# Mamba2 scan and PReLU block: pairs 2 to 5 in the half-and-half layout, and the last group's product 3 unsplit

## The chip, the cores and the metric

The kernel runs on one core of a Trainium2 chip. The metric is the device time of one execution in microseconds. The core's engines are TensorE (PE, with its weight loads as PEld), VectorE (DVE), ScalarE (ACT), GpSimd (POOL) and SyncE (SP, which here only issues transfers); sixteen DMA engines move data. Each engine has its own queue of instructions and waits for others by semaphores.

## The reference

Two stages follow each other. The first is a state-space scan with batch 4, 8 heads, 768 tokens, head size 32 and state size 16. The second takes the scan's result as 3072 tokens of 256 values through a hidden layer of 2048 with a two-sided PReLU.

```python
# first stage, per batch and head (run in chunks in the reference)
state = decay[t] * state + outer(B[t], x[t])
y[t]  = C[t] @ state
# bridge: (B,H,S,D) -> (B*S, H*D)
x = attn_out.transpose(0, 2, 1, 3).reshape(3072, 256)
h = x @ w_in                                       # 256 x 2048
g = np.maximum(h, 0.0) + alpha * np.minimum(h, 0.0)
return g @ w_out                                   # 2048 x 256
```

In chunked form a chunk's output is (C B^T, times a triangle of decays) x, plus the decayed C times the state at the chunk's start. The weights arrive in 64-bit floats.

## The kernel before

**Chunks and pairs.** The kernel uses chunks of Q = 128 tokens, 6 per batch, and works on two chunks at a time: pairs gp = 0 to 11, three per batch. For each pair it loads B, C and x (`nat`, `xt`), decays spread over partitions (`abc`, from rows that the kernel itself writes to a scratch in DRAM) and cumulated decays (`ap`). For one pair the steps are: transposes of B and C (`T`, L640), the products C B^T called gram (L702, L713), triangles of decays by scans on DVE (L532, L538), their product with gram (L724), the pair's share to the two states called added (L580, L595), the update of the states with a mask on POOL (L613, L616), and y (L750 to L758, L768 to L776), which ACT copies into `xT`, the tokens of the second stage.

**Two layouts.** Pairs 0 to 5 hold a whole chunk on all 128 partitions, one after the other. Pairs 6 to 11 (`gp >= HALF`) hold chunk k on half k of the partitions, in two blocks of 64 tokens. There the triangle needs only 192 columns per head (SQ) in place of 256, gram, y and added issue their matmuls in two halves of TensorE's rows, B and x are loaded in four transfers of 64 partitions (`load_tokens`, L146), and parts of C and the state have to be moved to the other half of the partitions (`moved`, L656, ACT L661 and POOL L663). The layout also wants the decay rows turned in a halved form: `rows_turn` (L443, copies at L457) does it for the second set of rows, which serves pairs 6 to 11. The first set, for pairs 0 to 5, is turned whole.

**Groups.** The second stage works on groups of 512 tokens, which are two pairs. Group 0 (pairs 0 and 1) is computed plainly by `hidden` (L996, ACT L999) and `output` (L1034) over 16 slices f of the hidden layer, while the weights arrive and are converted in pieces: raw on SP (L249), wt and wg on ACT (L265, L272, L275), POOL L267, DVE L286 and L296, and POOL L318 writes the finished piece. Its first four slices run as `hidden_two` (L1011) inside `first_two` (L792), the function that computes pairs 0 and 1. Groups 1 to 5 use a scheme of seven products in place of eight: `quad` (L1118) issues the first product (L1130), PReLU (L1113, L1115) and the second product (`product`, L1105), and calls `after(j)` between its steps.

**Order.** The order is written out by hand. Pairs 2 and 3 run in coarse steps within the loop over f from 4 to 15 of group 0; pairs 4 to 11 run in fine steps that `after(j)` places by its dictionary of steps in the quads. `load_next` and `load_pair` place the transfers on SP's queue, where pair 2's loads stand ahead of the fifth and later weight pieces. `keep_warm` (L326) issues matmuls of ones on TensorE, at the very start and where it would wait in `first_two`.

**State products.** For pairs 4 to 11, added of pair gp + 1 is put into unused columns of the banks of pair gp's y (`beside`). For pairs 2 and 3 it has a bank of its own and is issued ahead of gram, at the first of the coarse steps.

**The end.** In the last group, product 3 is computed with tokens on the partitions (L1097), in four matmuls of 128 columns per call and in two halves. `close` (L1218) then issues the products as 1, 2, 6, 5, 7, 4 and the halves of 3, with transposes (L1229) between them; the part `rest` that needs product 3 is transposed ahead of it, two adds on DVE (L1273) finish it, and `send` (L1235) stores each half in 64 KB.

## Time and profile before

| What | us |
|---|---|
| Three runs: lowest, median, highest | 359.12, 359.5, 359.89 |
| Profiled execution: its time and its span | 359.5, 357.8 |
| PE busy of the span | 350.7 (98%) |
| PEld | 288.2 (81%) |
| DVE | 239.4 (67%) |
| POOL | 205.3 (57%) |
| ACT | 173.7 (49%) |

The span is the time from the first to the last event of the profile; 1.7 us lie around it. The slices show each engine's busy share in tenths over 40 equal parts of the span. In a timeline a row gives the start, the time, the engine, the line, the operation with output and input, the shapes and how many instructions follow each other; in brackets is the idle time of the engine before it and what ended it. A group of matmuls is pipelined, so a row's end overlaps the next row's start.

### The profile page before, as it was taken

Reading aid. Unit: us, or ns where it says so; the run is one execution under the profiler, and the core shown is the slowest. Engines: PE = TensorE matmul, PEld = TensorE weight load, DVE = VectorE, ACT = ScalarE, POOL = GpSimd, SP = SyncE. Lnnn points to the kernel's source line nnn. Section 1 sums busy time; section 2 is a strip of 40 time slices with the busy share of each in tenths; the row PEclk is TensorE's granted clock in tenths of the full one; section 3 lists DMA queues with packets and bytes.
Section 4 is the critical chain, followed back from the end, with each engine's and each line's share of the span. In section 5 each row is a group of like instructions: output and inputs, shape, how many; then the busy total and the mean of one; then the engine's idle time right before and its main releaser. Section 6 shows DMA issues by size and latency. Waiting matters only on the chain.

```text
span 357.8 us, 7565 instructions
## 1 busy us (share of the span) xinstructions
PE 350.7 (98%) x2894; PEld 288.2 (81%) x2894; DVE 239.4 (67%) x467; ACT 173.7 (49%) x387; POOL 205.3 (57%) x221
## 2 busy tenths in 40 slices
PE   8899999999999999999999999999999999999995
PEld 7576666578888888888888888888888888888884
DVE  6987986998748756857747847757856633653263
ACT  3577666535355346346345445445445344444331
POOL 4886668589938855725645725647626535533520
PEclk9999999999999999999999999999999999999999
DMA  6989999508245403503413423413001002002004
GB/s 112 191 178 310 319 217 242 136 16 170 93 92 127 96 2 74 105 2 80 92 38 75 84 54 74 88 48 72 3 4 29 0 2 31 0 0 32 0 3 88
DMA packets 105469, 30.19 MB, mean 84 GB/s; under 512 B 79880, under 2 KB 101336, under 8 KB 105432
## 3 DMA queue, kind: packets, MB, share of 16 engines
q1 hardware_dynamic: 104360, 29.39, 37.3%
q8 instruction: 23, 0.38, 0.5%
q10 hardware_dynamic: 1072, 0.31, 0.4%
q14 instruction: 14, 0.11, 0.1%
HBM read 26.32 MB, written 3.37 MB: 83 GB/s over the span
## 4 chain that ended last, share of the span: by engine, by line
PE 85%; SPq 7%; DVE 3%; DMA 1%; ACT 1%; POOL 1%; issue 1%; ACTq 0%; DVEq 0%
PE bank L1105 32%; PE hp L1130 28%; PE bank L1034 6%; PE ss L1130 6%; PE hp L996 3%; SPq L188 3%; SPq L192 2%; PE ss L758 1%; DMA raw<-in_moe_w_in_dram 1%; DVE dec L538 1%; PE ss L702 1%; PE bank L1097 1%; PE ss L750 1%; PE ss L776 1%; DVE wr L296 1%
## 5 line engine op out<-in xcount | busy, mean ns | idle before, releaser
L1187 POOL TENSOR_TENSOR gt<-gt 128x512 f32<-128x512 f32 x58 | 74.2, 1278 | 21.1 <-DVE gt L1115 16.3
L1105 PE MATMUL bank<-gt,w_out 128*128 128x256 f32 x320 | 83.8, 382 | 0.2 <-DVE u L1248 0.2
L1105 PEld LDWEIGHTS bank<-gt,w_out 128*128 128x128 f32 x320 | 60.0, 190 | 9.7 <-issue 1.6
L1115 DVE SCALAR_TENSOR_TENSOR gt<-hp,s_mul,gt 128x256 f32<-128x256 f32 x96 | 42.0, 479 | 29.1 <-ACT gt L1113 26.9
L1177 POOL TENSOR_TENSOR gt<-gt 128x512 f32<-128x512 f32 x20 | 25.4, 1269 | 62.6 <-DVE gt L1115 50.2
L1113 ACT ACTIVATE gt<-hp,s_alpha 128x256 f32<-128x256 f32 x96 | 40.3, 471 | 34.6 <-PE hp L1130 31.5
L1105 PE MATMUL bank<-gt,ws 128*128 128x256 f32 x224 | 55.9, 379 | 0.0
L1105 PEld LDWEIGHTS bank<-gt,ws 128*128 128x128 f32 x224 | 42.3, 190 | 5.6
L1130 PE MATMUL hp<-xs,w_in 128*128 128x256 f32 x160 | 41.9, 384 | 0.0
L1130 PE MATMUL hp<-xs,ws 128*128 128x256 f32 x160 | 41.1, 380 | 0.0
L1156 DVE TENSOR_TENSOR hp<-hp,u 128x512 f32<-128x512 f32 x20 | 14.0, 700 | 35.8 <-ACT u L1154 35.8
L1130 PEld LDWEIGHTS hp<-xs,ws 128*128 128x128 f32 x160 | 30.3, 190 | 4.3 <-POOL xs L1075 0.2
L1130 PEld LDWEIGHTS hp<-xs,w_in 128*128 128x128 f32 x160 | 29.7, 190 | 4.4
L1034 PE MATMUL bank<-w_out,gt 128*128 128x256 f32 x128 | 31.1, 385 | 0.1
L1034 PEld LDWEIGHTS bank<-w_out,gt 128*128 128x128 f32 x128 | 23.6, 190 | 6.9 <-issue 2.9
L1130 PE MATMUL ss<-xT,w_in 128*128 128x256 f32 x96 | 24.6, 379 | 0.0
L996 PE MATMUL hp<-xT,w_in 128*128 128x512 f32 x48 | 22.7, 596 | 0.1
L616 POOL TENSOR_TENSOR sm<-state,bmask 128x256 f32<-128x256 f32 (+1 forms) x10 | 6.2, 619 | 28.9 <-DVE state L613 28.9
L532 DVE TENSOR_TENSOR_SCAN dec<-abc,bank 128x192 f32<-128x192 f32 x48 | 22.7, 523 | 0.0
L1145 ACT COPY m<-hp 128x512 f32<-128x512 f32 x8 | 4.7, 586 | 35.7 <-PE hp L1130 35.7
L1154 ACT COPY u<-hp 128x512 f32<-128x512 f32 x20 | 11.7, 586 | 19.4 <-PE hp L1130 19.4
L1115 DVE SCALAR_TENSOR_TENSOR gt<-c,s_mul,gt 128x256 f32<-128x256 f32 x40 | 20.5, 554 | 0.0
(204 smaller groups left out, 617.4 us busy)
## 6 DMA issues: line engine op xcount, KB each, us to landing
abc<-z SPq DMA_DIRECT2D x24, 192.0 KB
raw<-in_moe_w_in_dram SPq DMA_DIRECT2D x8, 512.0 KB
raw<-in_moe_w_out_dram SPq DMA_DIRECT2D x8, 512.0 KB
abc<-z SPq DMA_DIRECT2D x8, 512.0 KB
out_dram<-o_sb SPq DMA_DIRECT2D x33, 64.0 KB
nat<-in_B_dram SPq DMA_DIRECT2D x26, 64.0 KB
nat<-in_C_dram SPq DMA_DIRECT2D x24, 64.0 KB
xt<-in_x_dram SPq DMA_DIRECT2D x12, 128.0 KB
```

Of the source, the lines that this page charges most:

```text
L188: nc.sync.dma_start(out=nat[:, i, k].rearrange("p (h n) -> p h n", h=H), in_=src[b, :, ts, :].rearrange("h p n -> p h n"))
L532: nc.vector.tensor_tensor_scan(out=dv[:, o : o + SQ], data0=abc[k][:, s : s + SQ], data1=ident_p[0][:, :SQ], initial=0.0, op0=ALU.mult, op ...
L996: nc.tensor.matmul(hp, w_in[:, k, f * P : (f + 1) * P], xts[g][:, k], start=(k == 0), stop=(k == KC - 1))
L1034: nc.tensor.matmul(pos[0][t // 2][:, t % 2], gt[:, t * Q : (t + 1) * Q], w_out[:, f], start=(f == 0 and t % 2 == 0), stop=(f == NF - 1), s ...
L1105: nc.tensor.matmul(ms[g][i][:, h], w, blocks[g, z][n][:, p], start=(q == 0 and h == 0), stop=(q == NQ - 1), skip_group_check=True)
L1113: nc.scalar.mul(o[:, p], h[:, p], s_alpha[:, fs[p]])
L1115: nc.vector.scalar_tensor_tensor(out=o[:, p], in0=h[:, p], scalar=s_mul[:, fs[p]], in1=o[:, p], op0=ALU.mult, op1=ALU.max)
L1130: nc.tensor.matmul(to[:, p], w(2 * z + p), b, start=start and p == 0, stop=True, skip_group_check=True)
L1154: nc.scalar.copy(out=u2, in_=A)
L1156: nc.vector.tensor_tensor(out=Y, in0=Y, in1=u2, op=ALU.add)
L1177: nc.gpsimd.tensor_tensor(out=tc_, in0=g22, in1=g12, op=ALU.subtract)
L1187: eng.tensor_tensor(out=o, in0=x0, in1=x1, op=ALU.subtract)
```

## The change

Pairs 2 to 5 take the layout of pairs 6 to 11; pairs 0 and 1 stay whole, with a loader of their own (`load_whole`).

- Loads: B and x of pairs 2 to 5 in four transfers each, the spread of decays of every later pair as two transfers into one tile of 1536 columns, which has two buffers.
- Row products: the first set is turned twice in `first_two`, whole for pairs 0 and 1 and halved for pairs 2 to 5. The halved form is written by four matmuls into the upper half of the bank `hp`, four ACT copies take it out, and four calls of `keep_warm`, in place of six, follow in the same bank. The second set is turned by four matmuls as well, so the two ACT copies that swapped its halves go. DVE copies the ends of the rows.
- The identity that the scans use is halved where it is made, ahead of pair 2, and no longer ahead of pair 6.
- Pairs 2 and 3: added stands right behind gram, in unused columns of the gram banks 2 and 3; the update of the states and the moved parts follow it.
- The transposes of B turn a token block at a time, and ACT copies them out in two parts.
- The end: product 3 is two matmuls of 256 columns per call again, as the other products are. `close` issues 1, 2, 5, 6, 7, 4, 3 without transposes between them and then three blocks of transposes, copy (ACT, ACT, DVE) and store of 128 KB; one of the sums moves to POOL.

```diff
-    lda = ctx.enter_context(tc.tile_pool(name="lda", bufs=3))
+    lda = ctx.enter_context(tc.tile_pool(name="lda", bufs=2))
...
-        for w, t in enumerate(loads["p", gp][1] if gp >= HALF else ()):
-            rows = scratch["z", b // 2].rearrange("(b h c) t -> b c h t", b=2, h=H)
-            for k in range(2):
-                nc.sync.dma_start(
-                    out=t[HQ * k : HQ * (k + 1), : 4 * SQ].rearrange("p (h t) -> p h t", h=4),
-                    in_=rows[b % 2, c + k, 4 * w : 4 * w + 4].unsqueeze(0)
-                    .to_broadcast([HQ, 4, SQ]))
-        for k, t in enumerate(loads["p", gp][1] if gp < HALF else ()):
-            rows = scratch["z", b // 2].rearrange("(b h c) t -> b c h t", b=2, h=H)[b % 2, c + k]
-            nc.sync.dma_start(out=t.rearrange("p (h t) -> p h t", h=H),
-                              in_=rows.unsqueeze(0).to_broadcast([P, H, Q]))
+        rows = scratch["z", b // 2].rearrange("(b h c) t -> b c h t", b=2, h=H)[b % 2]
+        for k in range(2):
+            nc.sync.dma_start(
+                out=loads["p", gp][1][HQ * k : HQ * (k + 1)].rearrange("p (h t) -> p h t", h=H),
+                in_=rows[c + k].unsqueeze(0).to_broadcast([HQ, H, SQ]))
...
     def load_pair(gp, decays=True):
...
+        nat, abc, xt, ap = pair_tiles(gp)
+        if gp >= NB:
+            load_heads(ap, "pf", b, c)
+        load_tokens(nat[:, 0], B[b], c * Q)
+        if gp > GC:
+            for i, src in enumerate((B, C)):
+                load_blocks(nat, i, src[b], c * Q)
+        else:
+            load_chunks(nat[:, 1], C[b], c * Q)
+        load_tokens(xt, x[b], c * Q)
+        if decays:
+            load_spread(gp, b, c)
...
         nc.scalar.copy(out=m5_bank[0][:, HT:], in_=ident_h[:, :HT])
+        for s in range(2):
+            nc.scalar.copy(out=m5_bank[0][HQ:, HT:].rearrange("p (a s t) -> p s a t", a=2, s=2)[:, s],
+                           in_=ident[HQ:, HQ * (1 - s) : HQ * (2 - s)].unsqueeze(1)
+                           .to_broadcast([HQ, 2, HQ]))
         ident_p.append(m5_bank[0][:, HT:])
 
...
+    def rows_ends(i, eng=nc.vector):
+        d0 = held[i]
+        eng.tensor_copy(out=d0[:, Q + 1 :], in_=d0[:, HQ + 1 : Q])
...
-    def rows_turn(i, pr):
-
-        ps = ss_tile() if i else ps_s.tile([P, 512], F32, name="ss")
+    def rows_turn_whole(pr):
+
+        ps = ps_s.tile([P, 512], F32, name="ss")
         nc.tensor.transpose(ps[:, :RW], pr, ident[:RW, :RW])
-        if i == 0:
-            nc.tensor.transpose(ps[:, RW : RW + NF], al_n, ident[:NF, :NF])
-        else:
-            nc.tensor.transpose(ps[:, RW : 2 * RW], held["prs"], ident[:RW, :RW])
-        t = bat.tile([P, RW], F32, name="prt")
-        if i == 0:
-            nc.scalar.copy(out=t, in_=ps[:, :RW])
-        for v in range(2 if i else 0):
+        nc.tensor.transpose(ps[:, RW : RW + NF], al_n, ident[:NF, :NF])
+        t = prep.tile([P, RW], F32, name="prt")
+        nc.scalar.copy(out=t, in_=ps[:, :RW])
+        nc.scalar.copy(out=alpha, in_=ps[:, RW : RW + NF])
+        prt["whole"] = t
+
+    def rows_turn(i, pr, ps):
+
+        for v in range(2):
+            for s in range(2):
+                j = s ^ v
+                nc.tensor.matmul(ps[HQ * v : HQ * (v + 1), s * RW : (s + 1) * RW],
+                                 pr[:, HQ * j : HQ * (j + 1)], ident[:RW, :RW], start=True,
+                                 stop=True, tile_position=(0, HQ * v), skip_group_check=True)
+        if i:
+            rows_copy(i, ps)
+
+    def rows_copy(i, ps):
+
+        t = bat.tile([P, RW], F32, name="prh")
+        for v in range(2):
             vs = slice(HQ * v, HQ * (v + 1))
             for j in range(2):
                 nc.scalar.copy(
                     out=t[vs].rearrange("p (j b m h) -> p j b h m", j=2, b=2, h=H)[:, j],
                     in_=ps[vs, (j ^ v) * RW : ((j ^ v) + 1) * RW]
                     .rearrange("p (b h m k) -> p k b h m", b=2, h=H, k=2)[:, v])
-        if i == 0:
-            nc.scalar.copy(out=alpha, in_=ps[:, RW : RW + NF])
         prt[i] = t
...
+    def dps_of(gram):
+        return [gram[2 + k][:, 2 * SQ + 2 * D * k : 2 * SQ + 2 * D * (k + 1)] for k in range(2)]
...
+        def move_states():
+            for k, (to, frm) in enumerate(others):
+                if st[k] is not None:
+                    nc.gpsimd.tensor_copy(out=moved_s[to], in_=st[k][frm])
...
+            for k, (to, frm) in enumerate(others):
+                nc.scalar.copy(out=moved_c[to], in_=cd[frm, k])
...
+        else:
+            products_of_c()
+            scan_heads(dec, abc, 0, 2)
+            yield
+            scan_heads(dec, abc, 2, 2)
+            yield
+        small = 2 if fine else 3
+        gram = {r: ss_tile() if r < small else spare() for r in range(4)}
+        gram_products(bc, cz, gram)
+        if not fine:
+            dps = dps_of(gram)
+            added(dps, bn, xt, nk)
+            states(dps)
+            move_states()
...
+        for i in range(2):
+            for q in range(4):
+                qs = slice(32 * q, 32 * q + 32)
+                for k in range(2):
+                    ks, w = slice(HQ * k, HQ * (k + 1)), k ^ i
+                    if st[k] is not None:
+                        nc.tensor.matmul(y[k][qs, w], (moved_s if i else st[k])[ks, qs],
+                                         moved_c[ks] if i else cd[ks, k], start=i == 0,
+                                         stop=False, tile_position=(HQ * k, 32 * q),
+                                         skip_group_check=True)
+        x_products(y, xt, dec, [s is not None for s in st])
...
-        rows_turn(0, pr)
+        rows_turn_whole(pr)
...
         hp = spare()
-        keep_warm(hp, 6, Q)
+        rows_turn(0, pr, hp[:, 2 * Q :])
+        rows_copy(0, hp[:, 2 * Q :])
+        keep_warm(hp, 4, Q)
...
-        if g == NG - 1 and n == 3:
-            for s in halves:
-                ts = slice(s * P, (s + 1) * P)
-                for p in parts:
-                    q = 2 * z + p
-                    nc.tensor.matmul(ms[g][i][:, h, ts], blocks[g, z][n][:, p, ts], s4[:, q],
-                                     start=(q == 0 and h == 0 and s == 0), stop=(q == NQ - 1),
-                                     skip_group_check=True)
-            return
...
         for n in (1, 2):
             product(g, NZ - 1, n)
         nc.scalar.copy(out=sa[:, 0], in_=m[1])
         add(out=c[0][:, 0], in0=m[2], in1=sa[:, 0], op=ALU.add)
-        turn(g, 0, c[0], slice(0, HT), [nc.sync, nc.scalar])
-        product(g, NZ - 1, 6)
-        add(out=u[:, 0], in0=m[6], in1=sa[:, 0], op=ALU.add)
         product(g, NZ - 1, 5)
         nc.scalar.copy(out=sa[:, 1], in_=m[5])
-        add(out=c[0][:, 1], in0=u[:, 0], in1=sa[:, 1], op=ALU.add)
-        product(g, NZ - 1, 7)
+        turn(g, 0, c[0], slice(0, HT), [nc.sync, nc.scalar])
+        for n in (6, 7):
+            product(g, NZ - 1, n)
+        add(out=u[:, 0], in0=m[6], in1=sa[:, 0], op=ALU.add)
         add(out=u[:, 1], in0=m[7], in1=u[:, 0], op=ALU.add)
+        nc.gpsimd.tensor_tensor(out=u[:, 0], in0=u[:, 0], in1=sa[:, 1], op=ALU.add)
         add(out=c[1][:, 1], in0=u[:, 1], in1=sa[:, 1], op=ALU.add)
-        ps = [ps_h.tile([P, 512], F32, name="turned", tag="hp") for i in range(2)]
-        turned(c[0][:, 1], ps[0])
-        rest = tokens()
-        nc.scalar.copy(out=rest.rearrange("p b m -> p (b m)"), in_=ps[0][:, :HT])
         product(g, NZ - 1, 4)
         add(out=c[1][:, 0], in0=u[:, 1], in1=m[4], op=ALU.subtract)
-        turned(c[1][:, 1], ps[1])
-        o = tokens()
-        nc.scalar.copy(out=o.rearrange("p b m -> p (b m)"), in_=ps[1][:, :HT])
-        send(1, 1, o, nc.sync)
-        product(g, NZ - 1, 3, halves=(0,))
-        ps = ps_s.tile([P, 512], F32, name="turned", tag="ss")
-        turned(c[1][:, 0], ps)
-        o = tokens()
-        nc.scalar.copy(out=o.rearrange("p b m -> p (b m)"), in_=ps[:, :HT])
-        send(1, 0, o, nc.scalar)
-        product(g, NZ - 1, 3, halves=(1,))
-        for b in range(2):
-            add(out=rest[:, b], in0=m[3][:, b * P : (b + 1) * P], in1=rest[:, b], op=ALU.add)
-            send(0, 1, rest, (nc.sync, nc.scalar)[b], (b,))
+        product(g, NZ - 1, 3)
+        store(1, 1, ps_h, nc.scalar.copy, nc.sync)
+        store(1, 0, ps_h, nc.scalar.copy, nc.scalar)
+        add(out=c[0][:, 1], in0=m[3], in1=u[:, 0], op=ALU.add)
+        store(0, 1, ps_s, nc.vector.tensor_copy, nc.sync)
...
-    beside[GC] = m5_bank[0][:, : 2 * Q]
+    beside[GC] = m5_bank[0], bank(2)
...
-                    rows_turn(1, held["pr"])
+                    rows_turn(1, held["pr"], ss_tile())
```

## The prediction, made before the changed kernel ran

> **What bounds the kernel now.** I read the page first (slices of busy share), then a table by stretches, then TensorE's own timeline around the parts that change.
>
> ```profile
> span 357.8 us, 7565 instructions
> PE   8899999999999999999999999999999999999995
> ...
> 28.60:46.60 18.00, 17.89 (x80) 10.88 (x80) 15.42 (x27) 11.65 (x23) 11.68 (x13) 1.00 1.00 301
> 46.60:90.00 43.40, 43.40 (x310) 30.66 (x311) 36.62 (x64) 25.04 (x50) 33.02 (x34) 1.00 0.69 160
> ```
>
> The last two lines are: stretch, length, busy time of PE, PEld, DVE, ACT, POOL, granted clock, DMA share, GB/s. From 46.6 PE is busy in every microsecond of the rows up to 345; from 28.6 to 46.6 in 17.89 of 18.00. So in the body only TensorE's issue time counts. Ahead of 28.6 and behind 345 it waits for others. The profiled execution took 359.5 us, 1.7 more than its span, and is itself the median of the three runs; I sum against 359.5.
>
> The start:
>
> ```profile
> 0.82 3.75 PE L326 MATMUL hp<-const-float32-1.0 128*128 128x128 f32 x16 [0.82 <-PEq L1452]
> 7.38 1.50 PE L326 MATMUL hp<-const-float32-1.0 128*128 128x128 f32 x12
> 8.20 0.91 ACT L813 ACTIVATE cz<-bc,par 128x256 f32<-128x256 f32 x2
> 9.16 0.48 PE L822 MATMUL ss<-cz,bc 32*128 32x256 f32 x2 [0.28 <-ACT cz L813]
> 11.13 1.28 POOL L851 TENSOR_TENSOR dec<-o_sb,dec 128x512 f32<-128x512 f32 x1
> 19.08 1.27 POOL L318 TENSOR_TENSOR w_in<-wr,wg 128x512 uint32<-128x512 uint32 x1 [0.69 <-DVE wr L296]
> ...
> L457 ACT COPY prt<-ss x4: 240/242/245, 117.6 to 118.0; 64x48 f32<-64x48 f32 x4
> ```
>
> The first gram starts 0.05 us behind cz, in step with ACT. The last line, ACT's group of copies, is an operation that the change also puts here.
>
> Body, TensorE alone. Calls of 128x256 follow each other at 0.863 us per four, so the stretch that a pair's small products take is: start of the call before, plus its issue time, up to the start of the call behind.
>
> ```profile
> 40.76 1.02 PE L996 MATMUL hp<-xT,w_in 128*128 128x512 f32 x2
> 42.79 0.48 PE L1034 MATMUL bank<-w_out,gt 128*128 128x256 f32 x1
> ...
> 145.93 1.03 PE L1105 MATMUL bank<-gt,ws 128*128 128x256 f32 x4
> 147.72 0.70 PE L1105 MATMUL bank<-gt,w_out 128*128 128x256 f32 x2
> ...
> 124.74 1.03 PE L1105 MATMUL bank<-gt,w_out 128*128 128x256 f32 x4
> 127.69 1.13 PE L1130 MATMUL hp<-xs,w_in 128*128 128x256 f32 x4
> ...
> 206.34 1.03 PE L1105 MATMUL bank<-gt,w_out 128*128 128x256 f32 x4
> 209.05 0.48 PE L1130 MATMUL hp<-xs,w_in 128*128 128x256 f32 x1
> ```
>
> Whole gram (pair 2): 42.79 - 41.62 = 1.17. Halved: 147.72 - 146.79 = 0.93. y with the next pair's two states, whole (pair 5): 127.69 - 125.60 = 2.09; halved: 209.05 - 207.20 = 1.85.
>
> **The change, part by part**
>
> *Gram, y and states of pairs 2 to 5 (PE).* By the same reading, in us, whole against halved rows. Pair 2: gram 1.17, its one state alone 0.34, y 1.69; now 0.93, the state right behind other products 0.25, y alone 1.51 (the y at 288.66): gain 0.51. Pair 3: 1.18 + 0.45 + 1.48 against 0.93 + 0.33 + 1.50: gain 0.35. Pair 4: gram 1.33 (it waited 0.16) and y with one state 1.81, against 0.93 and 1.76: 0.45, or 0.29 if the wait stays. Pair 5: 0.24 + 0.24 = 0.48. Against this, turning the second set of row products takes four 64x96 matmuls for two transposes, about 0.30 for 0.17: loss 0.15 with the extra start. Sum 1.64, of which 0.33 (pair 2's gram and state) lies ahead of 46.6: **-1.3 behind 46.6** (bounds -1.0, -1.5) and **-0.33 ahead**.
>
> *DVE.* A halved pair scans 8 x 192 (0.47 each) instead of 8 x 256 (0.58) and multiplies 384 columns (0.55) instead of 512 (0.68): 1.4 us less per pair. DVE is not the bound, but the chain of waits in 28.6 to 46.6 runs through pair 2's scans (2.33 at 36.99 and at 41.10) to the w_out piece at 45.28 to 46.56, for which PE idled 0.26. Those scans become 0.45 shorter each: **-0.26**, not more, since PE is dense ahead of it.
>
> *Start: wait added.* The program now turns the first row products twice: TensorE writes the halved form into the hp bank, four ACT copies (64x48) read it, and the keep-warm matmuls, in the same bank, must wait for the last copy. Behind them in TensorE's queue stands the first gram, and for the gram wait DVE's multiply, two ACT copies of it and POOL's multiply L851. ACT is at cz to 9.11; four copies at 0.24 with overlap, 0.69 by the group's row: 9.80. Keep-warm shrinks from 12 to 8 instructions, 8 x 0.125 = 1.0: gram at 10.8 instead of 9.16, +1.65. DVE was at scans until 10.72 and gram takes 1.13: its multiply moves from 10.63 to 11.95, +1.3. POOL was free at 11.05 and gets its copied gram at 12.55, +1.4. From there both are full: between 10 and 20 DVE is busy 9.90 of 10, POOL 8.90, and w_in's pieces (POOL at 16.34 and 19.08) hang on both; TensorE is busy 8.42 of 8.60 from 20 to 28.6. Nothing gives it back: **+1.3**. Bounds: 0 if it were absorbed, +1.65 if all goes through. ACT's identity copies for the halves, now ahead of pair 2 (two, 0.27 each), two moved_c copies per pair (0.30 each) and POOL's moved_s copies (two for pairs 2, 4 and 5, one for pair 3, 0.29 each) lie in idle time (ACT idles 6.3 and POOL 6.3 of the 18.0 from 28.6); without that cover, ACT's four there would hold up the conversions by 1.1.
>
> *Loads.* SP issues four more loads per pair (x and B in four parts of 64 partitions, 0.63 each by the existing halved pairs): 2.5 us per pair. For pair 2 they stand ahead of w_in's piece issued at 25.84. But SP already stands still for 4.24 us at 19.68 with the DMA engines full, so the part ahead of that is free: w_in's piece about 1.1 later, no more than its users, which the start delays by 1.3. The spread of decays falls from 1 MB to 0.77 MB per pair. I take **0**; bounds -0.4 (0.26 MB less at 301 GB/s is 0.85, half of it felt) and +1.2 (all 2.5 felt, less the 1.3 by which the users come later).
>
> *Last group.*
>
> ```profile
> 348.12 1.89 PE L1105 MATMUL bank<-gt,ws 128*128 128x256 f32 x8
> 350.20 1.10 PE L1105 MATMUL bank<-gt,w_out 128*128 128x256 f32 x4 [0.19 <-DVE u L1248]
> 351.94 1.03 PE L1105 MATMUL bank<-gt,w_out 128*128 128x256 f32 x4
> 353.76 0.61 PE L1097 MATMUL bank<-ws,gt 128*128 128x128 f32 x4
> 354.36 0.99 ACTq L1235 DMA_DIRECT2D out_dram<-o_sb  x2
> ```
>
> Product 3 as two matmuls of 256 costs 0.865 instead of 0.89 in each of three earlier calls: **-0.08**. In the close, products 5, 6, 7, 4, 3 now run unbroken, 348.12 + 5 x 0.863 = 352.44; the add of product 3 (0.42, half product behind it 0.2) ends at 353.08, the transposes at 353.58, DVE's copy (0.40) at 354.02, and the last store issues at 354.05 instead of 354.98 (the second of ACT's pair above). It carries 128 KB, not 64: +0.2. **-0.7** (bounds -1.0 with no such loss, +0.2 if the sums before product 3 hold it up).
>
> **Sum:** +1.3 - 0.33 - 0.26 - 1.3 - 0.08 - 0.7 = -1.37: 359.5 to **358.1 us**.
>
> Two rules of the Trainium skill bear on this, and nothing above or below rests on them. "DMA: Bandwidth & Descriptors", Rules for kernel authors, advises against two transfers to disjoint partition halves and for one of 128 partitions; by it the 2.5 us of issue buys nothing, and with none of it hidden the sum would be 359.3 (the loads' upper bound) instead of 358.1. "TensorE: Matmul & The Clock Gate", What's actually happening, gives half rate after an idle window of about 3.4 us; the new idle stretch of TensorE, about 8.0 to 9.8, is shorter, so by it the clock rival below would not come, and where the free-running window falls no row here shows.
>
> **Rivals**
> - *The start's delay is absorbed.* Then +0.3 at most, 357.1 or less. For it: POOL idles 0.69 ahead of 19.08. Against: DVE has no gap there.
> - *Conversions bind in 28.6 to 47* (loads late, or ACT standing behind POOL's cd, at 37.92 to 38.65, before w_in's next piece): +1.2 by either (the loads' upper bound; ACT's conversion at 37.50 started at 38.65), **359.3**, no change that can be told. For it: DMA share 1.00 there, and PE already lost 0.26 to a w_out piece.
> - *The close gives nothing:* +0.9, 359.0.
> - *Slower: TensorE's clock falls* in the new idle stretch. The first 16 warm-up instructions took 0.234 each, the later 12 took 0.125: at the start TensorE runs at half rate for about 3.75 us. If 1.8 us of idling brings that back, keep-warm (1.0), gram (1.13) and the state product behind it (0.35) take twice as long: +2.3 on the sum to 2.5, **360.4 to 360.6**. It decides from +2.1. Against: keep-warm is still there, and PE is busy ahead of the gap.
>
> **How the numbers follow.** This kernel's measurement tells 0.2%, 0.72 us, from no change: faster is below 358.8, slower above 360.2. The sum as it stands 0.50 (own range 357.3 to 358.9), absorbed 0.12, conversions 0.17 (0.02 of it, at half its price, still faster), close 0.06, clock 0.10, an unseen stall 0.05. Faster: 0.46 + 0.12 + 0.02 = 0.60. Same: 0.04 + 0.15 + 0.06 + 0.01 = 0.26. Slower: 0.10 + 0.04 = 0.14. Range 356.8 to 360.4: it leaves out the lower half of "absorbed" and part of the clock and the stalls.
>
> **What the new profile would show.** Start: keep-warm behind an ACT copy, PE idle near 8.0 to 9.8, gram near 10.8, first w_in products near 19.0 instead of 17.66, the call at 28.61 near 29.9. Each gram of pairs 2 to 5 at 0.93; no state product of its own for pairs 2 and 3; PE dense behind 48. Last store issued 0.9 nearer to the last product. Wrong if the call at 28.61 stays put, if PE has gaps of over 0.5 us between 30 and 90, or if keep-warm rows read 0.23 each.

## The result: slower by 0.9%, and the profile after

The changed kernel takes **362.47 us** (median of 4 runs, 362.04 to 363.22) against 359.31 for the kernel before beside it (359.12 to 359.89): ratio 1.0087, interval 1.0066 to 1.0108. The forecast was 358.1 with a range to 360.4, so the time went the other way and left the range. The profiled execution took 362.44, span 360.7, so it stands for the median.

The page of the changed kernel (span, busy time, slices of TensorE, the chain of waits by engine):

```profile
span 360.7 us, 8061 instructions
PE 351.6 (97%) x3128; PEld 289.0 (80%) x3128; DVE 233.4 (65%) x467; ACT 175.9 (49%) x399; POOL 210.0 (58%) x229
PE   7999999899999999999999999999999999999996
...
PE 76%; SPq 7%; POOL 5%; DVE 5%; ACT 2%; issue 2%; DMA 1%; POOLq 0%; DVEq 0%; ACTq 0%
```

The table by stretches (length, busy time of PE, PEld, DVE, ACT, POOL, granted clock, that is the share of TensorE's full clock that it was given, DMA share, GB/s):

```profile
28.60:46.60 18.00, 17.86 (x107) 11.37 (x106) 13.20 (x26) 13.09 (x28) 10.54 (x12) 1.00 1.01 289
46.60:90.00 43.40, 41.87 (x410) 28.65 (x409) 33.26 (x63) 23.86 (x50) 34.67 (x38) 1.00 0.62 125
```

TensorE's share in the chain fell from 85% to 76%. Its row is no longer dense behind 46.6: 1.53 us of the 43.40 idle, where before not one hundredth was. DVE is less busy than before, as planned, and ACT 1.4 us busier in the first stretch.

To see where the time came from, I follow the same call in both traces (start after minus start before):

| what stands there | before | after | offset |
|---|---|---|---|
| first w_in call of the hidden block that I used as a mark | 28.61 | 29.94 | +1.33 |
| call ahead of pair 2's gram | 39.90 | 40.79 | +0.89 |
| call behind pair 2's gram and states | 44.62 | 46.23 | +1.61 |
| call ahead of pair 3's gram | 61.52 | 62.34 | +0.82 |
| call behind pair 3's gram and states | 66.28 | 69.02 | +2.74 |
| first products with ws (second group) | 80.12 | 83.50 | +3.38 |
| behind pair 5's gram | 120.32 | 124.00 | +3.68 |
| behind pair 5's y | 127.69 | 131.43 | +3.74 |
| in the close, the eight matmuls of products 5 and 6 | 348.12 | 351.76 | +3.64 |
| end of the span | 357.8 | 360.7 | +2.9 |

The small products did get cheaper (the offset falls between the rows on pairs 2 and 3), but gram of pairs 2 and 3 each *lost* time, 0.72 and 1.92 us with the wait behind it. Up to the first ws products 0.64 more is lost, from there to the end of pair 5's y 0.36, and the close takes 0.7 back. The start came as forecast. TensorE's and ACT's timeline of the start:

```profile
8.82 0.67 ACT L462 COPY prh<-hp 64x48 f32<-64x48 f32 x4
9.54 1.16 PE L324 MATMUL hp<-const-float32-1.0 128*128 128x128 f32 x8 [1.70 <-ACT prh L462]
10.63 0.48 PE L775 MATMUL ss<-cz,bc 32*128 32x256 f32 x2
18.99 1.99 PE L968 MATMUL hp<-xT,w_in 128*128 128x256 f32 x8 [0.83 <-POOL w_in L316]
29.94 1.95 PE L953 MATMUL hp<-xT,w_in 128*128 128x512 f32 x4
```

Keep-warm stands behind the four copies (1.70 us idle), gram starts at 10.63, the first w_in products at 18.99 and the marked call at 29.94: forecast were 10.8, 19.0 and about 29.9. Now the same timeline around gram of pair 2 and of pair 3:

```profile
37.63 1.27 POOL L316 TENSOR_TENSOR w_out<-wr,wg 128x512 uint32<-128x512 uint32 x1 [0.87 <-ACT gt L956]
38.85 0.73 POOL L678 TENSOR_TENSOR cd<-bc,ap 128x256 f32<-128x256 f32 x1
39.62 0.62 ACT L681 COPY moved_c<-cd 64x128 f32<-64x128 f32 x2 [1.21 <-POOL cd L678]
41.50 0.67 ACT L956 ACTIVATE gt<-hp,s_alpha 128x512 f32<-128x512 f32 x1
42.45 0.75 DVE L957 SCALAR_TENSOR_TENSOR gt<-hp,s_mul,gt 128x512 f32<-128x512 f32 x1
42.60 0.45 PE L586 MATMUL ss<-cz,bc 32*64 32x256 f32 x4
43.25 0.43 PE L586 MATMUL hp<-cz,bc 32*64 32x256 f32 x2
44.40 1.99 PE L991 MATMUL bank<-w_out,gt 128*128 128x256 f32 x8
...
61.42 0.73 POOL L678 TENSOR_TENSOR cd<-bc,ap 128x256 f32<-128x256 f32 x1
62.19 0.60 ACT L681 COPY moved_c<-cd 64x128 f32<-64x128 f32 x2 [3.33 <-POOL cd L678]
63.94 0.67 ACT L956 ACTIVATE gt<-hp,s_alpha 128x512 f32<-128x512 f32 x1
64.15 0.45 PE L586 MATMUL ss<-cz,bc 32*64 32x256 f32 x4
64.64 0.75 DVE L957 SCALAR_TENSOR_TENSOR gt<-hp,s_mul,gt 128x512 f32<-128x512 f32 x1 [2.14 <-ACT gt L956]
65.45 0.43 PE L586 MATMUL hp<-cz,bc 32*64 32x256 f32 x2 [0.62 <-DVE gt L957]
66.63 1.99 PE L991 MATMUL bank<-w_out,gt 128*128 128x256 f32 x8
69.02 1.98 PE L953 MATMUL hp<-xT,w_in 128*128 128x512 f32 x4 [0.40 <-DVE gt L957]
```

Read it as one chain. POOL's multiply into cd stands behind POOL's w_out piece (38.85; 61.42). The new moved_c copies stand in ACT's queue *ahead* of the call's PReLU and wait for cd: ACT idles 1.21 and then 3.33 us. PReLU (L956) and its second half on DVE (L957) are late, so the hp bank that they read comes free late. One of gram's four banks is that hp bank: TensorE begins gram in the other three and waits for the fourth, which DVE leaves at 43.20 and 65.39. From gram's start to the call behind it are 1.80 us for pair 2 and 2.48 for pair 3; before it was 1.08 for each, for pair 3 from the first to the second of these rows:

```profile
63.33 0.48 PE L713 MATMUL bank<-cz,bc 32*128 32x256 f32 x1
64.41 2.00 PE L1034 MATMUL bank<-w_out,gt 128*128 128x256 f32 x8
```

The close begins on TensorE with this row:

```profile
351.76 1.89 PE L1052 MATMUL bank<-gt,ws 128*128 128x256 f32 x8
```

From products 5 and 6 to the span's end are 8.94 us, 9.68 before.

### The profile page after: what moved, and what is told of

The parts are those of the page before. It is cut to its first block, busy times and chain, and to the rows that moved or that the text cites. A ratio compares the mean times of both kernels' runs of the same rounds, so it can differ in the third digit from the quotient of the medians.

```text
span 360.7 us, 8061 instructions
## 1 busy us (share of the span) xinstructions
PE 351.6 (97%) x3128; PEld 289.0 (80%) x3128; DVE 233.4 (65%) x467; ACT 175.9 (49%) x399; POOL 210.0 (58%) x229
## 4 chain that ended last, share of the span: by engine, by line
PE 76%; SPq 7%; POOL 5%; DVE 5%; ACT 2%; issue 2%; DMA 1%; POOLq 0%; DVEq 0%; ACTq 0%
PE bank L1052 33%; PE hp L1077 28%; PE ss L1077 6%; PE bank L991 3%; SPq L215 2%; PE ss L606 2%; POOL w_out L316 2%; SPq L145 2%; PE ss L586 2%; PE ss L731 1%; DMA raw<-in_moe_w_in_dram 1%; POOL wt L265 1%; DVE wr L294 1%; DVE dec L529 1%; DVE gt L957 1%
## 5 line engine op out<-in xcount | busy, mean ns | idle before, releaser
L1052 PE MATMUL bank<-gt,ws 128*128 128x256 f32 x240 | 59.5, 379 | 0.0
L1052 PEld LDWEIGHTS bank<-gt,ws 128*128 128x128 f32 x240 | 45.6, 190 | 6.2
L529 DVE TENSOR_TENSOR_SCAN dec<-abc,bank 128x192 f32<-128x192 f32 x80 | 37.8, 527 | 2.8 <-DMA abc<-z 2.8
L1111 DVE TENSOR_TENSOR c<-hp,m 128x512 f32<-128x512 f32 x20 | 13.8, 692 | 10.6 <-PE hp L1077 10.6
```

Of the source, the lines that this page charges most:

```text
L529: nc.vector.tensor_tensor_scan(out=dec[:, h], data0=abc[:, h * SQ : (h + 1) * SQ], data1=ident_p[0][:, :SQ], initial=0.0, op0=ALU.mult, op ...
L1052: nc.tensor.matmul(ms[g][i][:, h], w, blocks[g, z][n][:, p], start=(q == 0 and h == 0), stop=(q == NQ - 1), skip_group_check=True)
L1111: nc.vector.tensor_tensor(out=c22, in0=A, in1=m5, op=ALU.add)
```

## The experiments

Four causes could be in it. **Theory 1**: ACT's moved_c copies hold PReLU, and so the hp bank and gram. **Theory 2**: in 28 to 47 the weight pieces set the pace, through the loads (more of them, on one queue), so that whatever is saved ahead is lost there. The others are the start's wait by itself, and an end that gives nothing. All runs were timed in five rounds beside the kernel before (its medians: 359.24, 359.45, 359.60, 359.17 in the four batches, e1 to e4, e5 to e8, e9 to e11 and e12). Each batch ran on another chip, so differences between batches are taken from the ratios.

**e1_late_copies: Theory 1 alone.** The two copies of pairs 2 and 3 are issued behind gram and the states.

```diff
+        def move_c():
+            for k, (to, frm) in enumerate(others):
+                nc.scalar.copy(out=moved_c[to], in_=cd[frm, k])
...
-            for k, (to, frm) in enumerate(others):
-                nc.scalar.copy(out=moved_c[to], in_=cd[frm, k])
+            if fine:
+                move_c()
...
             move_states()
+            move_c()
```

> The changed kernel with one step moved: for pairs 2 and 3 ACT's two moved_c copies are issued behind gram and the states, not right behind POOL's cd. The copies themselves stay. In the changed kernel ACT stood still for 1.21 us (pair 2) and 3.33 us (pair 3) waiting for cd with these copies at the head of its queue. Theory 1 (ACT's wait for POOL's cd holds up PReLU, which holds the hp bank that gram needs): the idle time of ACT ahead of these copies goes, gram with the state products of pair 2 falls from 1.80 to about 1.1 us and of pair 3 from 2.48 to about 1.2, the 0.40 wait of the following first product goes, and the time falls by 1.8 to 3.0 us, from 362.5 to about 359.5 to 360.7. Theory 2 (the hp banks are late because loads and conversions are late: SP's four more loads per pair, or DVE): gram of both pairs still waits as long, and the time stays within 0.7 us of 362.5.

Measured: 360.69 (359.26 to 362.11), ratio 1.0040 (1.0027 to 1.0053), 1.8 us less than the changed kernel. TensorE and ACT around the two grams in e1's timeline:

```profile
42.69 0.45 PE L586 MATMUL ss<-cz,bc 32*64 32x256 f32 x4
42.73 0.43 PE L586 MATMUL hp<-cz,bc 32*64 32x256 f32 x2
43.88 1.99 PE L996 MATMUL bank<-w_out,gt 128*128 128x256 f32 x8
44.68 0.62 ACT L677 COPY moved_c<-cd 64x128 f32<-64x128 f32 x2
...
66.36 1.88 PE L958 MATMUL hp<-xT,w_in 128*128 128x512 f32 x4
```

The hp part of gram now starts 0.04 us behind the first, and the call that started at 69.02 starts at 66.36, 0.08 behind the kernel before. Nothing but the place of the copies was changed, so Theory 1 is shown, for about 1.8 us of the median. In the profiled execution, which was e1's fastest run, the two stretches lose 0.11 and 0.10 where they lost 0.72 and 1.92. The spread of 2.9 us is new, and 1.4 us above the kernel before stays.

**e2_own_bank: the start alone.** Keep-warm goes first, and the halved rows are turned into the tp bank.

```diff
         hp = spare()
-        rows_turn(0, pr, hp[:, 2 * Q :])
-        rows_copy(0, hp[:, 2 * Q :])
         keep_warm(hp, 4, Q)
+        rows_turn(0, pr, tp[:, 2 * Q :])
+        rows_copy(0, tp[:, 2 * Q :])
```

> The changed kernel with the halved turn of the first row products written into the bank of the transposes of pair 0, after its copy, and behind the keep-warm matmuls in TensorE's queue; the four ACT copies stay where they are. So no keep-warm matmul waits for ACT. Theory 1 (the wait of keep-warm for the copies shifts everything by 1.3): the first gram starts near 9.0 instead of 10.75, the call of the fourth slice near 28.6 instead of 29.94, and the time falls by 1.0 to 1.4, to about 361.2. Theory 2 (the start's delay is taken up later, since loads are late by about as much): the start is early but the gap reappears ahead of 50, and the time stays within 0.5 of 362.5.

Measured: 362.31 (361.39 to 362.51), ratio 1.0078 (1.0064 to 1.0092): only 0.16 less. Gram starts at 9.00 and the marked call is 0.43 behind the kernel before instead of 1.33, but e2's timeline of TensorE gives it back:

```profile
36.44 1.88 PE L953 MATMUL hp<-xT,w_in 128*128 128x512 f32 x4
39.20 1.99 PE L991 MATMUL bank<-w_out,gt 128*128 128x256 f32 x8 [0.88 <-POOL w_out L316]
41.03 1.45 PE L953 MATMUL hp<-xT,w_in 128*128 128x512 f32 x3
```

The offset is -0.02 at 36.44 and +1.13 at 41.03. TensorE, earlier, stands there for a w_out piece, as Theory 2 has it.

**e3_both: e1 and e2 together.**

```diff
+            move_c()
...
-        rows_turn(0, pr, hp[:, 2 * Q :])
+        rows_turn(0, pr, tp[:, 2 * Q :])
```

> Both edits, the late copies and the halved turn in a bank of its own place. If the two delays add: the sum of both gains, 2.8 to 4.4 us below the changed kernel, 358.1 to 359.7. If the second edit's gain is hidden behind late loads once the first is gone, or the other way round: no better than the better one of the two by more than 0.5.

Measured: 360.27 (358.57 to 362.18), ratio 1.0028 (1.0012 to 1.0045). Against e2, taking the bank wait out is worth 2.0; against e1, the start is worth 0.4. It is still 1.0 slower than before, without the start's wait and without pair 3's at the bank. Other waits are left, and TensorE, which is earlier, meets them (e3's timeline):

```profile
38.31 1.99 PE L996 MATMUL bank<-w_out,gt 128*128 128x256 f32 x8 [0.44 <-POOL w_out L316]
42.35 0.43 PE L586 MATMUL hp<-cz,bc 32*64 32x256 f32 x2
81.14 1.10 PE L1082 MATMUL hp<-xs,ws 128*128 128x256 f32 x4 [0.45 <-DVE gt L962]
```

The w_out piece is late, and pair 2's gram, begun at 41.95, gets its hp bank at 42.35 and takes 1.56 us, where e1's took 1.19. So something else costs too, and it must outweigh the savings.

**e4_old_end: the changed kernel with the former product 3 and close.**

```diff
+        if g == NG - 1 and n == 3:
+            for s in halves:
+                ts = slice(s * P, (s + 1) * P)
+                for p in parts:
...
+        turned(c[0][:, 1], ps[0])
+        rest = tokens()
...
-        store(1, 1, ps_h, nc.scalar.copy, nc.sync)
```

> The changed kernel with the end of the kernel before: product 3 in four matmuls of 128 columns with tokens on the partitions and the close with transposes between the products. Theory 1 (the new end gains what the traces say, 0.74 in the close and 0.08 in product 3): the time rises by 0.6 to 1.0, to about 363.3. Theory 2 (the close gives nothing, and the shorter tail of the profile is another order of stores): within 0.3 of 362.5.

Measured: 363.77 (363.70 to 364.36), ratio 1.0129 (1.0116 to 1.0143), 1.3 more than the changed kernel. It is no clean price of the end: e4's table by stretches shows a lower granted clock (the number behind the five busy times) in the start, which this edit does not touch:

```profile
8.00:10.00 2.00, 0.43 (x2) 0.43 (x3) 2.00 (x3) 1.48 (x7) 1.22 (x6) 0.72 0.98 273
10.00:14.00 4.00, 4.00 (x40) 2.98 (x39) 0.95 (x2) 0.31 (x1) 1.03 (x1) 0.50 0.91 209
14.00:16.00 2.00, 2.00 (x31) 1.83 (x23) 1.92 (x4) 1.95 (x5) 1.64 (x2) 0.58 0.78 82
```

Keep-warm takes 2.08 us in it for 1.16 in the changed kernel, and the marked call is at +3.28. That is 1.95 more than the changed kernel's, of which 1.0 is left at the end of the first group (+3.76 for +2.74). So the end's share of the 1.3 is about 0.3, an estimate from one profiled execution.

**e8_before_new_end: the end from the other side**, the kernel before with the new product 3 and close alone.

```diff
-        if g == NG - 1 and n == 3:
-            for s in halves:
...
-        turned(c[0][:, 1], ps[0])
-        rest = tokens()
...
+        store(1, 1, ps_h, nc.scalar.copy, nc.sync)
```

> The kernel before with the new end alone: product 3 in two matmuls of 256 columns and the close with all products ahead of the transposes. From the trace (0.74 in the close, 0.08 in product 3) 358.4; from the run with the old end put back (1.3) 358.0. Rival: the close depends on what comes ahead of it, and the gain is under 0.4.

Measured: 359.09 (358.48 to 361.01), ratio 0.9993 (0.9980 to 1.0006). The median gains 0.36, which the interval does not tell from zero. Why not the trace's 0.74: in its profiled run (360.56) the last store's bytes ended some 4.5 us behind its issue, 2.8 in that of the kernel before. What delays them is not settled.

**e6_before_split: the count of loads alone.** The kernel before, with each load of B and x of pairs 2 to 5 split into two of 64 partitions, the same bytes.

```diff
-                nc.sync.dma_start(out=xt[:, k].rearrange("p (h d) -> p h d", h=H),
-                                  in_=x[b, :, ts, :].rearrange("h p d -> p h d"))
+                for v in range(2) if gp >= NB else (slice(None),):
+                    vs = slice(HQ * v, HQ * (v + 1)) if v in (0, 1) else v
+                    nc.sync.dma_start(out=xt[vs, k].rearrange("p (h d) -> p h d", h=H),
+                                      in_=x[b, :, ts, :][:, vs].rearrange("h p d -> p h d"))
```

> The kernel before with each load of B and x of pairs 2 to 5 split into its two halves of the partitions: four more issues on SP per pair, the same bytes to the same places, and the whole layout kept. Theory 1 (the number of loads costs): SP issues the piece of w_in that stood at 25.84 about 1.3 later, the decays of pair 3 (46.74) some 3 us later, scans or conversions wait, and the time rises by 0.5 to 2 above 359.3. Theory 2 (SP stands still there anyway, the loads are hidden, as the prediction had it): within 0.4 of 359.3.

Measured: 361.22 (360.45 to 361.83), ratio 1.0047 (1.0033 to 1.0060): **1.8 us slower** than its kernel before. SP's queue of e6, then its group of ACT's weight conversions (busy, mean ns, idle before, releaser):

```profile
20.78 4.42 SPq L196 DMA_DIRECT2D xt<-in_x_dram  x2
25.24 1.31 SPq L190 DMA_DIRECT2D nat<-in_B_dram  x2
28.58 0.62 SPq L253 DMA_DIRECT2D raw<-in_moe_w_in_dram  x1
52.06 1.25 SPq L160 DMA_DIRECT2D abc<-z  x2
```
```profile
L269 ACT ACTIVATE wt<-raw 128x512 f32<-128x512 f32 x16 | 10.8, 676 | 7.1 <-DMA raw<-in_moe_w_in_dram 6.5 <-DMA raw<-in_moe_w_out_dram 0.5
```

The same rows of the kernel before:

```profile
19.68 4.24 SPq L192 DMA_DIRECT2D xt<-in_x_dram  x1
23.96 0.58 SPq L188 DMA_DIRECT2D nat<-in_B_dram  x1
25.84 0.59 SPq L249 DMA_DIRECT2D raw<-in_moe_w_in_dram  x1
```
```profile
L265 ACT ACTIVATE wt<-raw 128x512 f32<-128x512 f32 x16 | 10.9, 680 | 2.9 <-DMA raw<-in_moe_w_in_dram 2.9
```

w_in's piece is issued 2.74 later and pair 3's decays 5.32 later (52.06 for 46.74), and ACT waits 7.1 us for raw weights instead of 2.9. Of the 2.74, 0.82 stands already ahead of pair 2's loads (17.89 for 17.07), where the edit changes nothing. The rest shows where extra issues are hidden and where they are not. Up to the second chunk's first load (25.24 for 23.96) two of the four extra issues cost only 0.46, since the stop in front of it takes part of them up: one transfer stands 3.74 us instead of 4.24. Behind the stop the other two cost 1.46, in full. The four of pair 3 come on top, and all that stands behind them in the queue moves.

**e5_two_loads: the changed kernel with B and x of pairs 2 to 5 in two loads of 128 partitions each**, so the count of loads as before.

```diff
-        load_tokens(nat[:, 0], B[b], c * Q)
+        if gp < NP // 2:
+            load_chunks(nat[:, 0], B[b], c * Q)
+        else:
+            load_tokens(nat[:, 0], B[b], c * Q)
```

> The changed kernel with B and x of pairs 2 to 5 loaded by two transfers of 128 partitions each, as in the kernel before, so that SP issues eight loads for a pair in place of twelve. The tokens then lie where the halved layout doesn't expect them: this run leaves the right order of tokens of pairs 2 to 5 out, and its output is another one; every other instruction and the bytes moved are as in the changed kernel. Theory 1 (SP's additional loads are a cost of their own: pair 2's loads and those of pair 3 go behind the weight pieces that they delay, scans wait 2.8 us for the decays): the scans' wait for abc falls under 1, and the time falls by 0.8 to 2, to 360.5 to 361.7. Theory 2 (only ACT's queue behind POOL's cd and the start count): within 0.5 of 362.5.

Measured: 362.75 (361.52 to 364.03), ratio 1.0088 (1.0066 to 1.0110). Inconclusive alone: in four of its six runs the mean granted clock was 0.989 to 0.995; the two at 1.0 took 361.52 and 361.65, about 0.9 under the changed kernel. The scans' wait for decays fell to 0.8 us, the sign that Theory 1 named, without a gain that can be told.

**e10_both_two_loads: the same on top of e3**, with neither the start's wait nor the bank's.

```diff
-        load_tokens(xt, x[b], c * Q)
+        if gp < NP // 2:
+            load_chunks(xt, x[b], c * Q)
```

> The run with two edits (late copies, halved turn in a place of its own) and B and x of pairs 2 to 5 in two transfers of 128 partitions in place of four of 64. This run leaves the right order of tokens of pairs 2 to 5 out. It asks the question of the loads again where neither ACT's queue nor an idle TensorE at the start hides it. If the number of loads costs what splitting cost the kernel before (1.8): 358.5 to 359. If not the number but the order (x ahead of the decays and the weight pieces) is what costs: within 0.5 of 360.3.

Measured: 358.07 (357.70 to 358.88), ratio 0.9960 (0.9945 to 0.9975), so 2.4 us less than e3 by the ratios, give or take 0.8. The profiled runs show where: from the marked call to the first ws products TensorE takes 50.91 us (29.17 to 80.08), in e3 52.55 (28.59 to 81.14), and from there to the span's end both take 277.0. The wait for the w_out piece that e3 has at 38.31 is gone in e10, and the one at the first ws products is 0.35 shorter. The scans' wait for decays, 2.4 us in e3 and 0.6 in e10, is not what costs: 1.93 of e3's stands at 97.55, behind the first ws products, where the two runs lose nothing against each other. Whether e10's time can be had with the tokens in order is open.

**e7_x_last: e3 with the same loads in another order**, x of pairs 2 and 3 behind the decays, and pair 2's behind two weight pieces as well.

```diff
-        load_tokens(xt, x[b], c * Q)
+        if gp >= 4:
+            load_tokens(xt, x[b], c * Q)
         if decays:
             load_spread(gp, b, c)
+        if gp == 3:
+            load_tokens(xt, x[b], c * Q)
...
         load_spread(2, *divmod(4, CPB))
+        load_tokens(loads["p", 2][2], x[0], 4 * Q)
```

> The run with both edits (late copies, halved turn in a place of its own) with one more step moved: for pairs 2 and 3 the four loads of x, which only the state products and y need, are issued behind the decays, and for pair 2 behind the two weight pieces. As many loads, in another order. If late weight pieces and decays are what took back the start's gain: ACT's waits for raw in 28 to 47 (2.1 and 1.55 us) fall to under 1, and the time falls by 0.7 to 1.5, to 358.8 to 359.6, with less spread from run to run. If the DMA engines' work is the limit and not the order: within 0.4 of 360.3.

Measured: 359.04 (358.05 to 361.58), ratio 0.9998 (0.9982 to 1.0015): 1.1 less than e3 by the ratios, give or take 0.8, without one load fewer. So a part of what the loads cost, by these medians about half, is what stands behind them in the queue. The sign that the expectation named did not come: in the profiled run ACT still waits 3.00 and 0.78 us for raw weights in 28 to 47, and 7.0 in all, as in e3. By which wait the order gains is not shown.

**e11_x_last_gap: e7 with the changed kernel's start again**, now that the loads bind less.

```diff
         hp = spare()
+        rows_turn(0, pr, hp[:, 2 * Q :])
+        rows_copy(0, hp[:, 2 * Q :])
         keep_warm(hp, 4, Q)
-        rows_turn(0, pr, tp[:, 2 * Q :])
-        rows_copy(0, tp[:, 2 * Q :])
```

> The run with late copies and x last, but with the start of the changed kernel, where keep-warm waits for four ACT copies. Against the run with all three edits (359.04) it prices the start alone, with the loads out of the way. If the start's shift counts in full once loads are earlier: 360.2 to 360.5. If later waits still take it up: within 0.4 of 359.0. In either case, if the idle stretch of TensorE is what lets its clock fall in some executions, some of these runs show a granted clock of 0.995 or less and are 1 to 2 us longer, and none of the run with all three edits did.

Measured: 360.31 (359.26 to 361.52), ratio 1.0016 (0.9998 to 1.0033), 1.27 over e7 by the medians and 0.65 by the ratios, whose intervals overlap. The 1.27 looks like the forecast's +1.3, but isn't it. In nine of the twelve runs the mean granted clock was 0.995 or less (median 360.96); the three others took 359.26, 359.28 and 359.51, against a median of 359.04 for e7. In the profiled run, one of these three, the marked call is at +1.54, and by the end of the first group the offset is +0.10 (+0.33 in e7): the delay is absorbed. By these three runs, what the start costs here is mostly the clock.

**e9_rest: e7 with two small edits more**, the copies into moved_c of pairs 4 and 5 late too, and the row ends written by max/min instead of a copy.

```diff
-        eng.tensor_copy(out=d0[:, Q + 1 :], in_=d0[:, HQ + 1 : Q])
+        eng.tensor_scalar(out=d0[:, Q + 1 :], in0=d0[:, HQ + 1 : Q], scalar1=1e-6, scalar2=1.0,
+                          op0=ALU.max, op1=ALU.min)
...
+                if fine and gp < NP // 2:
+                    move_c()
```

> The run with three edits (late copies, halved turn in a place of its own, x last) with two more: DVE's copy of the row ends (96x63) as the same max and min that the kernel before used, and the moved_c copies of pairs 4 and 5 behind their gram too. In the run before this one that copy took 1.30 us beside a POOL multiply, where the other form took 0.18, and TensorE's second product of the first quad waited 0.22 behind it; ACT stood 1.92 us at pair 5's cd in the changed kernel, and its gram took 1.21 in place of 0.84. If these are waits of their own: 0.3 to 0.7 less than with the three edits, 358.3 to 358.7, and the 96x63 operation under 0.4 us. If POOL's use of the shared port is what DVE waits for and not the form: the copy's time moves to the next operation and nothing changes, 358.8 to 359.3.

Measured: 358.51 (357.93 to 362.27), ratio 0.9984 (0.9963 to 1.0005). It is the best version that does the whole work, but it is told neither from the kernel before nor from e7. The form of the row ends gives nothing: the instruction takes 1.29 us as max/min too (1.30 as a copy). The copies of pairs 4 and 5 do what those of pairs 2 and 3 did: ACT's wait ahead of pair 5's (1.92 us for POOL's cd in the changed kernel) is gone, and pair 5's gram takes 0.99 us (118.73 to 119.72), where it took 1.19 to 1.21 in e1, e7 and the changed kernel. At the first ws products TensorE starts 1.11 us behind the call ahead, 1.09 in e7, 1.48 in the changed kernel and 0.87 before, so what was won there was won ahead of these two edits.

**e12_x_pool: e9 with x of pairs 2 and 3 issued by POOL** instead of SP, since SP's queue was the trouble.

```diff
-            load_tokens(xt, x[b], c * Q)
+            load_tokens(xt, x[b], c * Q, eng=nc.gpsimd)
...
-        load_tokens(loads["p", 2][2], x[0], 4 * Q)
+        load_tokens(loads["p", 2][2], x[0], 4 * Q, eng=nc.gpsimd)
```

> The run with five edits (358.51), and the eight loads of x of pairs 2 and 3 issued by POOL in place of SP: pair 2's in POOL's idle time of some 2.8 us at the start, pair 3's ahead of its cd. All tokens in their right places. With half as many tokens' loads on SP the run that left the right order out took 358.07 with two edits only. If SP's queue (its issue time and the loads that each waits for) is what the additional loads cost: 357.0 to 358.0, better than both kernels. If POOL's time for issuing them costs as much, or the DMA engines' work is the limit: 358.5 or more.

Measured: 361.85 (361.07 to 362.19), ratio 1.0071 (1.0056 to 1.0086), 3 us worse than e9. POOL's timeline:

```profile
3.81 2.94 POOL L145 DMA_DIRECT2D xt<-in_x_dram  x4
...
38.58 3.07 POOL L145 DMA_DIRECT2D xt<-in_x_dram  x4
41.66 0.74 POOL L686 TENSOR_TENSOR cd<-bc,ap 128x256 f32<-128x256 f32 x1
```

Four issues occupy POOL itself for 3 us, ahead of cd and the weight pieces. With the first four the marked call comes 1.8 later than in e9 (30.65 for 28.83); 1.0 of this is TensorE's longer wait for pair 0's C (1.13 for 0.16), so the early bytes of x may cost as well as POOL's time. The two are not separated.

## Why the prediction was wrong, point by point

Four kernels differ by one edit at a time, so their ratios, times 359.4, split the loss:

| kernel | ratio | step | us |
|---|---|---|---|
| e10: no bank wait, no start wait, loads of 128 partitions | 0.9960 | what the change saves (to before) | -1.4 |
| e3: with its loads | 1.0028 | the loads' count | +2.4 |
| e2: with ACT's copies in their place | 1.0078 | the bank wait | +1.8 |
| the changed kernel | 1.0087 | the start | +0.3 |

The steps add up to +3.1, the result, because each starts where the one before ends. Each carries the intervals of two ratios, about 1 us, so the start's 0.3 is not told from zero; e1 (1.8 for the copies) and e6 (1.8 for the loads, on the kernel before) give the middle two again on other ground. Another order would split it otherwise, since the start and the loads make the same pieces late for the same users: on the changed kernel itself, with its late start, e5's two runs at full clock gain 0.9. e10 with the changed kernel's start was not run. Against the forecast of -1.4 the result is 4.5 more: 1.8 for the bank, 2.4 for the loads, and 1.3 of the forecast savings (2.7 without start and loads) that did not come, less 1.0 for the start.

*"ACT's identity copies..., two moved_c copies per pair... lie in idle time"* is the step that failed worst: **+1.8** instead of 0. ACT's idle time was there. But an in-order queue does not put a copy into idle time; it puts it where it was issued, and there it waited for POOL and held PReLU behind it. I had even named "ACT standing behind POOL's cd" as a rival, and followed it to the conversions. I did not follow it to PReLU, to the bank that PReLU frees, and to gram, which takes that bank. The forecast's own sign of being wrong, gaps of TensorE of over 0.5 us between 30 and 90, came there: 0.62 ahead of 65.45. The price that I gave for lost cover, 1.1, was the copies' busy time; what counts is the wait ahead of them, 1.21 and 3.33.

*"Loads: I take 0"* failed too: **+1.8 to +2.4**, above the bound of 1.2. That SP stands still 4.24 us anyway did hide most of the issues ahead of the stop (0.46 for two in e6). But the term looked at pair 2 alone: w_in's piece is issued 1.71 later in the changed kernel (27.55 for 25.84; forecast 1.1), and pair 3's decays, behind two pairs' extra issues, 4.66 later (51.40 for 46.74), and these got no price. The bound took off 1.3 for users that the start made late, and that lateness is itself absorbed. The Trainium skill's "DMA: Bandwidth & Descriptors", Rules for kernel authors, speaks against two transfers to partition halves, and e6 bears it out on this kernel; by the loads' bound that I set beside that rule the sum was 359.3, and by e6's 1.8 it would have been 359.9.

*"Nothing gives it back: +1.3"*: the size was right in the trace (+1.33 at the mark), its effect on the end was not. e2 wins 0.16, e11's three runs above 0.995 lose about 0.25. Here the rival "the start's delay is absorbed" was the truth, though its total, 357.1, was not, and the absorber is another than I had looked for: not DVE or POOL in the start, but TensorE's wait for weight pieces at 36 to 41 and, in e3, for pair 2's bank, which are merely entered later.

*The clock rival* was given 0.10 and does not show in the profiled execution of the changed kernel (clock 1.00 throughout its start), so it does not explain the result; one of its four runs, 363.22, has a mean clock of 0.995. But it is real: see below.

*Gram, y and states of pairs 2 to 5*: right where nothing waits. Gram with the states behind it takes 1.19 for pair 2 and 1.22 for pair 3 in e1, where no wait stands in it (forecast 1.18 and 1.26), against the 1.80 and 2.48 of the changed kernel. Pair 2's y, from the call at 50.00 to the one at 55.46: 5.46 for 5.64, so 0.18 as forecast. The stretches ahead, out of which the state products went: 3.44 for 3.89 and 3.44 for 4.00, so 0.45 and 0.56 (forecast 0.34 and 0.45). Pair 4's gram 0.26 (0.24 to 0.40), its y 0.06 (0.05). Wrong for pair 5: its gram takes 1.21 from 122.79 to 124.00 (forecast 0.84, before 1.08), and y with the states 2.05 (before 1.99): 0.19 lost where 0.48 was forecast. The second turning of rows takes 0.49 instead of 0.30 (before 0.17). So the stretch from the first ws products to the end of pair 5's y, for which the forecast had -0.8 (0.45 + 0.48 - 0.15), gave +0.36, and most of the savings that did not come are here. A part of pair 5's is the same moved_c copies, put at nothing: with them behind gram, gram takes 0.99 in e9 and 0.98 in e12. The rest stays open.

*"PE idled 0.26" ahead of 46.56, gone*: hardly. The offset falls by 0.05 there, and the call at 48.17 still starts 1.94 behind the one ahead of it, for 1.98 before.

*The close, -0.7, and product 3, -0.08*: -0.74 and -0.10 in the trace, right in size, though e8's median gives 0.36 of it. The rival that it gives nothing is neither shown nor excluded.

## What to carry to other kernels

Before an instruction is costed at nothing because its engine has idle time, write down what it waits for and what stands behind it in that queue, and follow the first of those to the buffer that it frees and to who takes that buffer next. A DMA queue that stands still waiting for bytes hides only the issues ahead of the stop: in e6 those behind it cost their time in full, and everything queued behind them moved. When one delay is removed and nothing comes of it, look for the stage that now waits instead, and test the delay again after that stage is eased.

## What was not expected of the hardware

*The clock falls after an idle stretch of 1.7 us, sometimes.* In e4 TensorE was idle for 1.70 us ahead of keep-warm, and the granted clock was 0.72, 0.50 and 0.58 in 8 to 10, 10 to 14 and 14 to 16: worked out at half rate, from about 8.9 to 15.7, 6.8 us. The changed kernel has the same idle stretch and full clock. Over all executions of the five kernels with that stretch (the changed one, e1, e4, e5, e11) the mean clock was 0.995 or less in 23 of 38; of the five with that start mended (e2, e3, e7, e9, e10) in 1 of 48. The stretch is not its only cause: 3 of 6 in e12, whose start waits 1.13 for a load, and 3 of 17 in e6 and e8, with the former start. That the fall lies in the start is seen in the two profiled executions of e4 and e5 alone; in e8's it lies in the last 5 us (0.75 in 354 to 358), where TensorE has no work left, so a low mean alone does not show that products ran slower. The Trainium skill's "TensorE: Matmul & The Clock Gate", What's actually happening, has half rate after at least one idle window of about 3.4 us; these runs show it after half of that, and the measurement decides.

*A short DVE instruction can take seven times its time.* The row ends (96x63) took 0.18 us before, in another form and from another source; the timeline of DVE in the changed kernel:

```profile
79.12 1.30 DVE L407 COPY r<-r 96x63 f32<-96x63 f32 x1
81.15 1.42 DVE L422 TENSOR_TENSOR_SCAN rpf<-r,zeros 96x128 f32<-96x128 f32 x1
83.50 1.10 PE L1077 MATMUL hp<-xs,ws 128*128 128x256 f32 x4 [0.46 <-DVE gt L957]
```

In the kernel before it was the scan between these two that took 1.41 (0.77 here) and the last one 0.79. So one or another of the three is stretched, whichever meets something; TensorE then waits 0.46 for the DVE work behind them. What they meet was not tested.

*Spread.* e1, e3 and e7 vary by 2.9 to 3.6 us from run to run, where the kernel before beside them varies by 1.2 to 1.4. In e3 and e7 it isn't the clock (0.997 and more in all runs). e10, with fewer loads, varies by 1.2, which points to the loads, but was not pursued.
